# Where a block of normalised activations is written from and how it lies in SBUF, and who adds bias and x to the output, in a ConvNeXt-V2 block on one core

## The chip, the core and the metric

The kernel runs on one core of a Trainium2 chip. A core has five engines with a program each: TensorE (PE in the profile: matrix multiplies; PEld is its weight load), VectorE (DVE), ScalarE (ACT), GpSimd (POOL) and SyncE (SP, which here only issues transfers). They wait for each other through semaphores. Sixteen DMA engines carry transfers between HBM and SBUF, the on-chip memory of 128 partitions. A transfer is issued from the instruction queue of SP, ScalarE or GpSimd, and an instruction that waits holds up everything behind it in its queue. Matrix products land in PSUM, eight banks of 2 KB in each partition.

The metric is the device time of one execution in microseconds (us), the median of several.

## What is computed

One ConvNeXt-V2 block on an image of 512 x 512 pixels with 96 channels, in bfloat16, with 384 hidden channels:

```python
def reference(x, dw, w1, w2, grn_gamma, grn_beta):
    ...
    for i in range(K):
        for j in range(K):
            out = out + xp[:, i:i+H, j:j+W, :] * dw[i, j][None, None, None, :]
    h = _layernorm(out, axis=-1)
    h = jnp.einsum('bhwc,ce->bhwe', h, w1)
    h = _gelu(h)
    gx = jnp.sqrt((h * h).sum(axis=(1, 2), keepdims=True) + 1e-6)
    nx = gx / (gx.mean(axis=-1, keepdims=True) + 1e-6)
    h = grn_gamma * (h * nx) + grn_beta + h
    h = jnp.einsum('bhwe,ec->bhwc', h, w2)
    return x + h
```

The sum of `h * h` runs over the whole image, so nothing of the second product can be finished before every pixel has been through the first one. That cuts the kernel in two phases.

## The kernel before

**Tiles.** The image is cut into 128 blocks of 4 rows (`NBLK`, `GR`). A block is 2048 pixels. `yn` is the convolved and normalised block with rows x 32 channels on the partitions; `ynT` is the same block with channels on the partitions, and it is what the first product reads. The way from the one to the other leads through HBM: `stage_write` writes `yn` to `yn_dram` in four transfers, one for each row of the block, and `stage_read` reads the block back as 96 partitions of 4 KB. There is a ring of six `ynT` tiles; partitions 96 to 127 of them are set to zero once (`setup_ynt`), and so are those rows of the weights `w1p`, so that the product can run over 128 partitions.

**Phase 1** is a loop over slots; in a slot each step is done for another block, by a table (`put`, `get`). A block's way is: load x (`load_x`, four slots ahead), transpose on VectorE (`turn_x`), convolution on TensorE in three bursts (`conv`), evacuation by ScalarE (`evac`, the tile `y_bf`), squares on GpSimd (`stage_sq`), statistics on TensorE, inverse standard deviation for four blocks at a time on GpSimd (`stage_rstd`, `stage_newton`), its way through HBM to all partitions (`stage_rows`, `stage_bcast`), the normalisation on GpSimd (`stage_norm`, one slot later `stage_write`, another slot later `stage_read`), and two slots after that the first product with GELU. In that step `unit(bank, n)` makes n PSUM banks on TensorE and has ScalarE apply GELU from them into the tile `g`; ScalarE does nine such activations and one evacuation in a slot. VectorE then takes the statistics of `g` (BATCH_NORM_STATS2), TensorE the others (`gram_next`). The slots are called steady here when their block for the first product is below `TAIL0` (114).

In phase 1 SP issues all transfers of a slot, in this order: load of x, `stage_read`, `stage_write`, `stage_bcast`, `stage_rows`, and one third of a block of `g` that is kept in HBM (`store_next`). Every instruction on the engines stays in the order of the program (class `InOrder`, line 35, which is why most lines of the profile are L35).

**Phase 2** goes once more over the blocks. For 35 of them `g` is read back from HBM (`gl`, line 290, from GpSimd's queue), for 5 it was held in SBUF, and for 88 it is made again from `ynT` (`recompute`: three matmuls of 512 columns for each quarter of a block, one GELU of 1536 columns); for 85 of these `ynT` is read again from `yn_dram` (line 294, from SP's queue). That read takes 128 rows, the last 32 being the next block's, which meet zero weights. Then, for each block (`stage_mm2`):

- TensorE makes the second product in four parts (`sub`, 0 to 3) of 4 x 96 columns, 12 matmuls each. Two PSUM banks take turns (`out_bank`), so a part needs the bank of the part before the last.
- GpSimd has added x (`xr`, loaded by line 279) and the bias (`B2c`) for the whole block ahead of time (`stage_xb`, line 324, tile `xb`, two blocks ahead; three buffers).
- VectorE adds the PSUM bank and its part of `xb` into `o_sb` (four buffers), and SP stores `o_sb` when the next block is done (`stage_out`, line 352).

`pace` spreads the recomputed quarters evenly between the parts: about two for every three parts.

Of the kernel before, what the change touches and what calls it, by code (L numbers as in the profile page):

```python
# [12 lines left out]
GR = 4  # L13
# [43 lines left out]
def kernel(  # L57
# [52 lines left out]
    def chans(i):  # L110
        return slice(i, 64, 2) if i < 2 else slice(64, 96)
# [10 lines left out]
    def yn_src(q):  # L122
        return yn_dram[q].rearrange("c (r w) -> c r w", r=GR)

    def yn_rows(q):
        return yn_dram[q:q + 2].rearrange("q c (r w) -> (q c) r w", r=GR)[0:128]

# [10 lines left out]
    rowsel = consts.tile([128, GR], bf16, name="rowsel")  # L138
    w1_raw = consts.tile([C, E], bf16, name="w1_raw")
    w1p = consts.tile([128, E], bf16, name="w1p")  # L140
# [43 lines left out]
    with ExitStack() as p1:  # L184
# [68 lines left out]

        cen = consts.tile([C, 128], bf16, name="cen")
        xtpool = pc.enter_context(tc.tile_pool(name="xt", side="right", bufs=1))
# [27 lines left out]
        def load_rest(n, sq, pq):  # L283
            q = ORDER[n]
            v = grp.setdefault(q, {})
            if is_held(q):
                v["g"] = gs[q]
            elif is_whole(q):
                v["g"] = late.gl.tile([128, NQ, NCH, QW], bf16, name="gl")
                pq.dma_start(out=v["g"][:].rearrange("p t j w -> p (t j w)"), in_=g_dram[whole.index(q)])  # L290
            else:
                ynt = yn_ring[SLOTS[nth_made[q] % NYT]]
                if q not in KEPT:
                    sq.dma_start(out=ynt[:], in_=yn_rows(q))
                v["ynt"] = ynt
# [24 lines left out]
        def stage_xb(q, pq, bias):  # L320
            if q is None:
                return
            xb = late.xb.tile([128, PXP, C], f32, name="xb")
            pq.tensor_tensor(out=xb[:], in0=grp[q]["xr"][:],  # L324
                                    in1=bias[:, None, :].to_broadcast([128, PXP, C]), op=ALU.add)
            grp[q]["xb"] = xb

        def stage_mm2(n, q):
# [3 lines left out]
            for sub in range(NSUB):  # L332
                O = out_bank()
                for gl_ in range(GPS):
                    gg = sub * GPS + gl_
                    for j in range(NCH):
                        t, c = gg // GQ, gg % GQ * 128
                        pe.matmul(O[:, gl_, :], lhsT=g[:, t, j, c:c + 128], rhs=W2s[:, j, :],
                                   start=(j == 0), stop=(j == NCH - 1))
                dve.tensor_tensor(out=o_sb[:, sub * GPS:(sub + 1) * GPS, :], in0=O,  # L340
                                   in1=xb[:, sub * GPS:(sub + 1) * GPS, :], op=ALU.add)
                if n == NBLK - 1:
# [44 lines left out]
        pool.memset(cen[:], 1.0)  # L387
        pool.memset(w1p[C:128, :], 0.0)
        dve.memset(SG, 0.0)
# [24 lines left out]
        for i in range(NI):  # L414
            act.dma_start(out=w1_raw[i:C:NI, :], in_=w1[chans(i), :])
        act.dma_start(out=w2_sb[:], in_=w2.rearrange("(j p) c -> p j c", p=128))
# [4 lines left out]
        def setup_ynt():  # L421
            for t in yn_ring:
                pool.memset(t[C:128, :, :].rearrange("p r w -> p (r w)").bitcast(f32), 0.0)

        def setup_mlp():
# [6 lines left out]
            dve.scalar_tensor_tensor(out=w1p[:C, :], in0=w1m[:C], scalar=-1.0 / C, in1=w1_raw[:],  # L432
                                     op0=ALU.mult, op1=ALU.add)
# [207 lines left out]

        def stage_write(b):
            yn = yns.pop(b)
            for r in range(GR):
                sp.dma_start(out=yn_dst(b, r), in_=yn[32 * r:32 * r + 32, :, :])

        def stage_read(b):
            t = yn_ring[b % NYT]
            sp.dma_start(out=t[:C], in_=yn_src(b))
            ynts[b] = t  # L650
# [175 lines left out]
        for s in range(last_slot + 1):  # L826
            get = lambda kind: at.get((s, kind), [])
            if s + 4 < NBLK:
                load_x(s + 4)
            for b in get("read"):  # L830
                stage_read(b)
            for b in get("write"):
                stage_write(b)
            for k in get("bcast"):
                stage_bcast(k)
            for k in get("rows"):
                stage_rows(k)
            store_next()
            for k in get("newton"):
                stage_newton(k, pool)  # L840
# [4 lines left out]
            for k in get("rstd"):  # L845
                stage_rstd(k, pool)
            mlp = get("mlp")

# [36 lines left out]
            else:  # L885
# [4 lines left out]
                conv(0)  # L890
                unit(0, 2)
                unit(2, 1)
                squares(0)
# [4 lines left out]
                unit(3, 1)  # L898
                unit(4, 2)
                squares(1)  # L900
                gram_next(1 if taps else 2)
# [6 lines left out]
                if evac:  # L908
                    evac()
                gram_next(1 if taps else 2)  # L910
                unit(8, 2)
                unit(10, 1)
                for b2 in get("stats"):
# [138 lines left out]
```

## Time and profile before

| what | value |
|---|---|
| three runs | 1480.27, 1486.15, 1486.81 us |
| median of the runs | 1486.15 us |
| span of the profiled execution | 1480.8 us |
| mean granted TensorE clock in it | 0.994 of full speed |
| first matmul of the second product | 974.7 us after the start |
| moved by DMA | 433.08 MB, mean 292 GB/s |
| of it, reads of ynT in phase 2 | 85 of 512 KB |
| writes of yn | 512 of 96 KB |

The profile is that of one execution. Its page gives busy time for each engine and a line for each group of like instructions; the trace behind it has the start and length of every instruction, and from the semaphores it can be told who ended a wait. Busy time is a union: two overlapping instructions of an engine count once, and an engine that is busy all the time isn't always the one that the others wait for. Times within the trace count from its first instruction.

### The profile page before, as it was taken

How to read it: one execution, taken by the hardware profiler on the slowest of the kernel's cores; microseconds unless marked ns; L12 is line 12 of the kernel's file. 1: busy time of each engine (PE TensorE's matmuls, PEld its weight loads, DVE VectorE, ACT ScalarE, POOL GpSimd, SP SyncE). 2: the span in 40 equal slices, each digit the busy share in tenths (PEclk: the TensorE clock that was granted, in tenths of full speed). 3: DMA queues.
4: the chain of work that ended last, by engine and by line, in shares of the span. 5: the costliest groups of instructions: out<-in, count | busy, mean ns of one | idle time of the engine just before them, and what ended most of it. 6: DMA issues, size and time to landing. Idle time of an engine off the chain costs nothing.

```text
span 1480.8 us, 54225 instructions
## 1 busy us (share of the span) xinstructions
PE 1391.3 (94%) x23125; PEld 810.4 (55%) x23125; DVE 1182.0 (80%) x2135; ACT 1414.4 (96%) x1595; POOL 1300.3 (88%) x922
## 2 busy tenths in 40 slices
PE   8888999999999999999999997789999999999998
PEld 3434444444444444444444445467777777776776
DVE  7849989999999999999999987965555555555555
ACT  7888989999999999999999999999999999999997
POOL 3459889998998999998999987569999999999997
PEclk9999999999999999999999999999999999999999
DMA  5568788788888888888888866669999999999997
GB/s 180 179 205 255 241 253 280 228 271 260 260 248 264 258 264 255 276 253 254 263 258 266 263 216 195 195 225 409 366 359 402 417 416 413 419 410 417 411 412 282
DMA packets 167768, 433.08 MB, mean 292 GB/s; under 512 B 31558, under 2 KB 81318, under 8 KB 163046
## 3 DMA queue, kind: packets, MB, share of 16 engines
q1 hardware_dynamic: 151284, 326.04, 66.3%
q0 software_dynamic: 14880, 103.43, 17.6%
q8 instruction: 181, 2.97, 0.8%
q14 instruction: 61, 0.50, 0.1%
q10 hardware_dynamic: 1362, 0.15, 0.1%
HBM read 273.30 MB, written 156.22 MB: 290 GB/s over the span
## 4 chain that ended last, share of the span: by engine, by line
PE 30%; ACT 24%; DMA 19%; POOL 13%; DVE 6%; issue 4%; SPq 4%; POOLq 0%; ACTq 0%; DVEq 0%
PE PS L35 30%; ACT g L35 16%; DMA out_dram<-o_sb 9%; POOL yn L35 6%; ACT y_bf L35 5%; POOL ysq L35 5%; SPq L35 4%; DMA yn_dram<-yn 3%; DVE bst L35 3%; DMA xin<-in_x_dram 2%; DMA rbc<-r_dram 2%; DMA ynT<-yn_dram 1%; DMA g_dram<-g 1%; DVE o_sb L35 1%; ACT xT L35 1%
## 5 line engine op out<-in xcount | busy, mean ns | idle before, releaser
L35 ACT ACTIVATE g<-PS 128x512 bf16<-128x512 f32 (+2 forms) x1062 | 727.7, 864 | 16.5 <-PE PS L35 15.6
L35 DVE BATCH_NORM_STATS2 bst<-g 128x6 f32<-128x512 bf16 x1110 | 671.3, 672 | 35.4 <-ACT g L35 34.5
L35 PE MATMUL PS<-ynT,w1p 128*128 128x512 bf16 x2181 | 609.6, 381 | 23.6 <-ACT g L35 5.4
L35 ACT ACTIVATE gr<-PS 128x1536 bf16<-128x1536 f32 x360 | 498.5, 1459 | 18.8 <-PE PS L35 13.8
L35 POOL TENSOR_TENSOR yn<-y_bf,rbc 128x1536 bf16<-128x1536 bf16 x126 | 391.3, 3108 | 77.3 <-ACT rbc L35 21.9
L35 DVE TENSOR_TENSOR o_sb<-PS,xb 128x384 bf16<-128x384 f32 x512 | 277.3, 556 | 227.0 <-PE PS L35 190.1
L324 POOL TENSOR_TENSOR xb<-xr,B2c 128x1536 f32<-128x1536 bf16 x118 | 368.1, 3133 | 4.3 <-DVE o_sb L35 2.0
L35 PE MATMUL PS<-xT,Wq 64*32 64x511 bf16 (+1 forms) x9198 | 340.5, 389 | 26.2 <-ACT y_bf L35 8.1
L35 POOL TENSOR_TENSOR ysq<-y_bf 128x1536 bf16<-128x1536 bf16 x114 | 313.6, 2752 | 12.8 <-ACT y_bf L35 12.8
L35 PEld LDWEIGHTS <-w1p 128*128 128x128 bf16 x2181 | 171.6, 98 | 222.0 <-issue 133.4
L35 PEld LDWEIGHTS <-gr 128*128 128x128 bf16 x4296 | 212.1, 98 | 68.9 <-issue 12.0
L35 PE MATMUL PS<-W2s,gr 128*128 128x96 bf16 x4224 | 223.5, 206 | 8.2 <-DVE o_sb L35 8.0
L35 PEld LDWEIGHTS <-Wq 64*32 64x32 bf16 x9216 | 111.9, 90 | 193.3 <-issue 145.9
L35 ACT ACTIVATE y_bf<-PS 128x1536 bf16<-128x1536 f32 (+2 forms) x135 | 199.4, 1482 | 17.4 <-PE PS L35 13.3
L35 DVE STREAM_TRANSPOSE xT<-xin 128x576 f32<-128x576 f32 (+1 forms) x256 | 181.4, 748 | 8.1 <-DMA xin<-in_x_dram 8.1
L35 PEld LDWEIGHTS <-g 128*128 128x128 bf16 x1704 | 104.9, 98 | 86.3 <-issue 54.3
L35 PE MATMUL PS<-w1p,ynT 128*128 128x256 bf16 (+2 forms) x822 | 125.8, 273 | 8.0 <-ACT xT L35 3.2
L35 PE MATMUL PS<-g 128*128 128x128 bf16 x1464 | 122.6, 220 | 2.9 <-DVE PS L35 2.6
L35 PEld LDWEIGHTS <-gl 128*128 128x128 bf16 x1680 | 82.8, 98 | 26.8 <-issue 5.0
L35 PE MATMUL PS<-W2s,gl 128*128 128x96 bf16 x1680 | 89.5, 206 | 3.4 <-DVE o_sb L35 3.2
L35 PEld LDWEIGHTS <-ynT 128*128 128x128 bf16 x822 | 64.1, 97 | 31.5 <-issue 13.7
L279 POOL DMA_DIRECT2D xr<-in_x_dram x115 | 63.7, 555 | 14.2 <-POOL xb L324 14.2
(105 smaller groups left out, 576.5 us busy)
## 6 DMA issues: line engine op xcount, KB each, us to landing
xin<-in_x_dram SPq DMA_DIRECT2D x126, 432.0 KB
g_dram<-g SPq DMA_DIRECT2D x105, 512.0 KB
gl<-g_dram POOLq DMA_DIRECT2D x35, 1536.0 KB, 11.3
yn_dram<-yn SPq DMA_DIRECT2D x512, 96.0 KB
ynT<-yn_dram SPq DMA_DIRECT2D x128, 384.0 KB
out_dram<-o_sb SPq DMA_DIRECT2D x127, 384.0 KB
xr<-in_x_dram POOLq DMA_DIRECT2D x123, 384.0 KB, 6.9
ynT<-yn_dram SPq DMA_DIRECT2D x85, 512.0 KB
```

Of the source, the lines that this page charges most:

```text
L35: r = f(*a, **k)
L279: pq.dma_start(out=xr[:], in_=x[0, r0:r0 + GR].rearrange("r w c -> (r w) c").rearrange("(p g) c -> p g c", g=PXP))
L324: pq.tensor_tensor(out=xb[:], in0=grp[q]["xr"][:], in1=bias[:, None, :].to_broadcast([128, PXP, C]), op=ALU.add)
```

## The change

It has three parts.

1. **Layout of ynT.** Channel 3c+i goes to partition 4c+i instead of 3c+i. So three of every four partitions hold a channel and each fourth holds zero. A read is three transfers of 32 partitions (i = 0, 1, 2), in both phases; in phase 2 the next block's rows are no longer read. The weights `w1_raw` are laid out alike, and the ring's tiles are set to zero in all partitions.
2. **Queue of the writes.** In steady slots the four writes of `yn` are issued from ScalarE's queue, one each after the activations of unit(0, 2), unit(4, 2), the evacuation and unit(8, 2). SP's order in these slots becomes: load of x, broadcasts, rows, store, reads. In the other slots all stays on SP, reads first.
3. **The adds of phase 2.** GpSimd makes `xb` for the first three parts only. For the fourth VectorE first adds the bias to the PSUM bank in place, then adds x out of the bank into `o_sb`. `xr` is thus in use until VectorE's last add and has six buffers instead of five.

```diff
-    def yn_src(q):
-        return yn_dram[q].rearrange("c (r w) -> c r w", r=GR)
-
-    def yn_rows(q):
-        return yn_dram[q:q + 2].rearrange("q c (r w) -> (q c) r w", r=GR)[0:128]
+    def yn_src(q):
+        return yn_dram[q].rearrange("(c i) (r w) -> i c r w", i=NI, r=GR)
+
+    def read_yn(eng, t, q):
+        for i in range(NI):
+            eng.dma_start(out=t[i:128:4], in_=yn_src(q)[i])
...
                 if q not in KEPT:
-                    sq.dma_start(out=ynt[:], in_=yn_rows(q))
+                    read_yn(sq, ynt, q)
...
         def stage_xb(q, pq, bias):
-            xb = late.xb.tile([128, PXP, C], f32, name="xb")
-            pq.tensor_tensor(out=xb[:], in0=grp[q]["xr"][:],
-                                    in1=bias[:, None, :].to_broadcast([128, PXP, C]), op=ALU.add)
+            n = PXP - GPS
+            xb = late.xb.tile([128, n, C], f32, name="xb")
+            pq.tensor_tensor(out=xb[:], in0=grp[q]["xr"][:, :n, :],
+                                    in1=bias[:, None, :].to_broadcast([128, n, C]), op=ALU.add)
...
+                add = xb
+                if sub == NSUB - 1:
+                    dve.tensor_tensor(out=O, in0=O, in1=B2c[:, None, :].to_broadcast([128, GPS, C]), op=ALU.add)
+                    add = grp[q]["xr"]
                 dve.tensor_tensor(out=o_sb[:, sub * GPS:(sub + 1) * GPS, :], in0=O,
-                                   in1=xb[:, sub * GPS:(sub + 1) * GPS, :], op=ALU.add)
+                                   in1=add[:, sub * GPS:(sub + 1) * GPS, :], op=ALU.add)
...
-            act.dma_start(out=w1_raw[i:C:NI, :], in_=w1[chans(i), :])
+            act.dma_start(out=w1_raw[i:128:4, :], in_=w1[chans(i), :])
...
-                pool.memset(t[C:128, :, :].rearrange("p r w -> p (r w)").bitcast(f32), 0.0)
+                pool.memset(t[:].rearrange("p r w -> p (r w)").bitcast(f32), 0.0)
...
-        def stage_write(b):
+        def write_parts(b, eng):
             yn = yns.pop(b)
-            for r in range(GR):
-                sp.dma_start(out=yn_dst(b, r), in_=yn[32 * r:32 * r + 32, :, :])
+            return [lambda r=r: eng.dma_start(out=yn_dst(b, r), in_=yn[32 * r:32 * r + 32, :, :]) for r in range(GR)]
 
         def stage_read(b):
             t = yn_ring[b % NYT]
-            sp.dma_start(out=t[:C], in_=yn_src(b))
+            read_yn(sp, t, b)
...
-            for b in get("read"):
-                stage_read(b)
-            for b in get("write"):
-                stage_write(b)
+            mlp = get("mlp")
+            steady = bool(mlp) and mlp[0] < TAIL0
+            wparts = [f for b in get("write") for f in write_parts(b, act if steady else sp)]
+            if not steady:
+                for b in get("read"):
+                    stage_read(b)
+                while wparts:
+                    wparts.pop(0)()
...
             store_next()
+            if steady:
+                for b in get("read"):
+                    stage_read(b)
...
                 unit(0, 2)
+                write_next()
...
                 unit(4, 2)
+                write_next()
...
                 if evac:
                     evac()
+                write_next()
                 gram_next(1 if taps else 2)
                 unit(8, 2)
+                write_next(len(wparts))
...
-                late.xr = p2.enter_context(tc.tile_pool(name="xr", side="right", bufs=5))
+                late.xr = p2.enter_context(tc.tile_pool(name="xr", side="right", bufs=6))
```

More of the change, by code (lines that the diff above doesn't have):

```diff
@@ L138 @@
     rowsel = consts.tile([128, GR], bf16, name="rowsel")
-    w1_raw = consts.tile([C, E], bf16, name="w1_raw")
+    w1_raw = consts.tile([128, E], bf16, name="w1_raw")
     w1p = consts.tile([128, E], bf16, name="w1p")
@@ L252 @@
             dve.tensor_copy(out=eye32[32 * q:32 * q + 32, :], in_=ident_f[32 * q:32 * q + 32, 32 * q:32 * q + 32])
-        cen = consts.tile([C, 128], bf16, name="cen")
+        cen = consts.tile([128, 128], bf16, name="cen")
         xtpool = pc.enter_context(tc.tile_pool(name="xt", side="right", bufs=1))
@@ L387 @@
         pool.memset(cen[:], 1.0)
-        pool.memset(w1p[C:128, :], 0.0)
+        pool.memset(w1_raw[:], 0.0)
         dve.memset(SG, 0.0)
@@ L431, in setup_mlp @@
                           start=(j == 0), stop=(j == NCH - 1))
-            dve.scalar_tensor_tensor(out=w1p[:C, :], in0=w1m[:C], scalar=-1.0 / C, in1=w1_raw[:],
+            dve.scalar_tensor_tensor(out=w1p[:], in0=w1m, scalar=-1.0 / C, in1=w1_raw[:],
                                      op0=ALU.mult, op1=ALU.add)
@@ L838, with write_next @@
             store_next()
+            if steady:
+                for b in get("read"):
+                    stage_read(b)
+            def write_next(n=1):
+                for f in wparts[:n]:
+                    f()
+                del wparts[:n]
             for k in get("newton"):
@@ L846 @@
                 stage_rstd(k, pool)
-            mlp = get("mlp")
             def spread_out():
```

## The prediction, made before the changed kernel was run

> **What bounds the kernel now.** First the page's summary, then busy time in windows (start:end, then for each engine busy us and instruction count, TensorE clock, DMA share, GB/s): one from the steady part of phase 1, one from phase 2.
>
> ```profile
> PE 1391.3 (94%) x23125; PEld 810.4 (55%) x23125; DVE 1182.0 (80%) x2135; ACT 1414.4 (96%) x1595; POOL 1300.3 (88%) x922
> ...
> 300.00:360.00 60.00, 58.02 (x1058) 29.23 (x1056) 59.80 (x103) 60.00 (x86) 56.43 (x42) 1.00 0.82 256
> ...
> 1200.00:1260.00 60.00, 58.19 (x852) 42.96 (x850) 32.60 (x61) 57.29 (x42) 58.04 (x37) 1.00 1.02 414
> ```
>
> In phase 1 ScalarE has no idle time at all and VectorE 0.2 of 60 us: a slot (one block) lasts 7.03 us and ScalarE sets it. In phase 2 ScalarE, GpSimd, the DMA engines and TensorE all stand near full, VectorE at 54%. A busy share doesn't tell which one sets the end there, so I read the timeline (start, length, engine, operation):
>
> ```profile
> 1200.12 1.18 PE L35 MATMUL PS<-W2s,gl 128*128 128x96 bf16 x24
> ...
> 1200.84 1.07 DVE L35 TENSOR_TENSOR o_sb<-PS,xb 128x384 bf16<-128x384 f32 x2 [0.60 <-PE PS L35]
> ...
> 1201.14 0.81 PE L35 MATMUL PS<-ynT,w1p 128*128 128x512 bf16 x3
> ...
> 1201.79 0.67 PE L35 MATMUL PS<-W2s,gr 128*128 128x96 bf16 x12
> ...
> 1202.30 0.81 PE L35 MATMUL PS<-ynT,w1p 128*128 128x512 bf16 x3
> 1202.56 0.56 DVE L35 TENSOR_TENSOR o_sb<-PS,xb 128x384 bf16<-128x384 f32 x1 [0.66 <-PE PS L35]
> ...
> 1202.95 1.18 PE L35 MATMUL PS<-W2s,gr 128*128 128x96 bf16 x24
> ```
>
> From start to start TensorE takes 42.5 ns for a 96-wide matmul (1200.12 to 1201.14, 24 of them) and 216 ns for a 512-wide one (1201.14 to 1201.79, three), with nothing between. Phase 2 holds 6144 of the one and, after its first, 1038 of the other: 261 + 225 = 486 us. By the trace its matmuls run from 974.7 to 1477.1, 502.4 us. So **TensorE sets phase 2**, and some 16 us of it are waits. Which ones (waiter, what ended the wait, total us, times, longest):
>
> ```profile
> DVE o_sb L35 <- DMA out_dram<-o_sb: 35.4, 24, 2.7
> ...
> PE PS L35 <- DVE o_sb L35: 11.3, 15, 1.6
> ```
>
> VectorE waits for an output buffer whose store hasn't landed; the sum's PSUM bank stays full and TensorE stands still, 11.3 us in all. The DMA engines are full (1.02).
>
> **The change, part by part.**
>
> *Second add in phase 2.* In one part of four VectorE now adds the bias into the PSUM bank, then x out of it. The single add takes 0.556 us (group mean). No row has VectorE both reading and writing a 384-wide PSUM tile, so I take the same 0.556, and 0.034 us from the dependent chain of small VectorE operations at 969 to 971 us, where each starts that long after the end of the one it needs. The bank is held 0.59 us longer. VectorE has the time (128 x 0.556 = 71 us of some 230 idle), but there are two banks: the group after next needs this one. In the timeline above the pair at 1200.84 frees its first bank at 1201.40, and the group that needs it starts at 1201.79: slack 0.39. The add ending at 1203.12 frees a bank needed at 1203.46 (second half of the x24): 0.34. The second of the pair ends at 1201.91 for a group at 1202.95: 1.04. Taking from the trace all 127 last adds of a block against the group after next, 96 have 0.40 us or less and 31 have 1.05. Where TensorE does wait, it starts 0.053 us after the add's end (the smallest slack). So a wait of 0.59 + 0.053 - 0.398 = 0.245 us, 96 times: **+23.5 us**, on the engine that sets the end. Ends: 0.50 us (two adds at the pitch of an independent pair) gives +15; 0.75 (PSUM output a third dearer) gives +39. The last block's extra add lengthens the tail by **+0.6**.
>
> *Less for GpSimd.* Its add shrinks from 1536 to 1152 columns.
>
> ```profile
> L324 POOL TENSOR_TENSOR xb<-xr,B2c 128x1536 f32<-128x1536 bf16 x118 | 368.1, 3133 | 4.3 <-DVE o_sb L35 2.0
> ```
>
> With 0.30 us for 64 columns (var) as the other point, 1152 cost 2.39 us: 0.74 us less, 125 times. VectorE waits 0.9 us in all for xb, so this pays **0** by itself. Its worth is in what comes next: GpSimd's period is 3.95 us a block against TensorE's bare 486/128 = 3.80, so it would have capped any recovery. x is now held until VectorE's last add; a sixth buffer covers this, and GpSimd's load of x five blocks on waits for an event 1 us from the one its own add awaits now. **0**, ends 0 and +5.
>
> *Smaller reads in phase 2.* 85 reads go from 512 to 384 KB: 10.9 MB, 26 us at 416 GB/s, but only the 11.3 us of waits can be paid back. Per block the traffic becomes 189 MB/128 = 1.48 MB, in 4.0 us 370 GB/s against 416 at saturation, so I take the waits as gone: **-11.3**. Other end 0: each read becomes three issues on SP, and hardware DMAs take turns on eight semaphores (the trace shows the turn), so an issue waits for the landing of the eighth before it, now under three blocks back instead of five.
>
> *yn writes on ScalarE's queue.* 110 steady slots, 4 issues each. SP's row, and two from ScalarE's start-up:
>
> ```profile
> 312.05 2.49 SPq L35 DMA_DIRECT2D yn_dram<-yn  x4
> ...
> 5.59 0.59 ACTq L35 DMA_DIRECT2D w_raw<-in_w_dram  x1
> 5.77 0.88 ACT L35 ACTIVATE Wq<-g 32x288 bf16<-32x288 bf16 x2
> ...
> 11.63 0.38 ACTq L35 DMA_DIRECT2D bet_bf<-in_grn_beta_dram  x1
> 12.06 1.45 ACT L35 ACTIVATE y_bf<-PS 128x1536 bf16<-128x1536 f32 x1 [4.16 <-DMA gam_bf<-in_grn_gamma_dram]
> ```
>
> An issue takes 0.6 us of the queue. At 5.59 activations that stand ahead of it in the program run beside it: the queue goes on while the engine works. In the slot the four issues stand behind activations of 1024 or 1536 columns (0.9 and 1.33 us from start to start), so I cost them at **0**; the cover is 0.3 us each, and without it 440 x 0.6 = 264 us would fall on ScalarE. What isn't covered is a wait, as at 11.63: that issue waited for the semaphore last used by SP's load at 7.89, and ScalarE stood 4.16 us. Behind a waiting write stand all later activations, behind them TensorE's PSUM banks. (a) The first write needs yn. Setting the end of each yn against the start of the slot that will write it, yn is late in 30 of 108 slots: 5.9 us at worst near 115 us, later up to 3.9 and mostly under 1. Summed, 33 us beyond the cover; but a ScalarE that waits lets GpSimd (56 of 60 busy) catch up for good, so it is paid about once, and near 120 us the trace already has 4.9 us of ScalarE idle for the same lateness. **+1**, ends 0 and +33. (b) The shared semaphores: in slots with broadcasts the first write follows that slot's broadcast. **+2**, ends 0 and +25. The Trainium skill (DMA: Bandwidth & Descriptors, Anatomy of one DMA) states that a DMA's semaphore wait happens on the issuing sequencer before dispatch, so it speaks against a queue that sets the slot; if every late yn were paid, that rule would make (a) 33 instead of 1.
>
> *SP in phase 1* loses 2.5 us of issues a slot and gains two reads (0.7), and its broadcasts no longer stand behind writes that wait.
>
> ```profile
> SPq L35 <- DMA yn_dram<-yn: 133.5, 149, 3.8
> ...
> SPq L35 <- POOL yn L35: 64.3, 39, 4.2
> ```
>
> ScalarE's idle time from 240 to 900 us, beyond two gaps of its own, is 7 us (at 694 to 699 and 887 to 897, behind GpSimd). I take **-2**: ends -7 and 0.
>
> *Layout.* Three reads of 32 partitions for one of 96; the memset and the w1 setup keep their columns: **0**, since a read has two slots of lead. The skill (SBUF — State Buffer, Summary: rules for kernel authors) asks for 128 partitions and one DMA, not several; its fixed 2 us a DMA would make three reads in a row about 7 us by estimate, and that stays inside two slots, so the sum is the same by both.
>
> **Sum.** 23.5 + 0.6 - 11.3 + 1 + 2 - 2 = +13.8 on the profiled 1480.8: 1494.6. Three runs have 1480.27, 1486.15 and 1486.81, so the profiled execution is 5.3 below the median; the forecast is 1494.6 + 5.3 = **1500**.
>
> **Rivals.** *Faster:* the two adds end within 0.345 us of today's one (the slack less 0.053), so the banks don't bind, and both DMA waits and the 7 us in phase 1 go: 1486 - 11.3 - 7 = 1468. For it: full DMA engines, SP's long waits. Against: a second add of 0.556 us on a slack of 0.40. *No change:* the bank costs 15 and the waits go, with -2 to -7 in phase 1: 1486 + 15 - 11 - 4 + 1 = 1487. *ScalarE blocked:* writes wait once per four slots for yn or a broadcast, about 1 us in 27 groups, on top of the forecast: 1500 + 27 = 1527. For it: the 4.16 us at 12.06, and that late yn comes in every fourth slot. Against: paid-once lateness.
>
> **How the numbers follow.** About 0.5% (7 us) is what this kernel's runs can tell from no change. Forecast 0.47, ScalarE blocked 0.15, no change 0.19, faster 0.19. Slower 0.62, same 0.19, faster 0.19. Range 1470 to 1522: the low end near the faster rival, the high end the bank at +39 with the DMA waits gone, most of the blocked case's lower part in it; the forecast's own range is 1490 to 1512.
>
> **What would show it.** Right: in phase 2 two adds per last part, the second 0.03 us behind the first; TensorE's wait for VectorE up from 11 to over 20 us, in some 100 pieces of 0.25; waits for output stores nearly gone; DMA share under 0.95; GpSimd no longer full. In phase 1 slots of 7.03 us still, ScalarE's queue issuing beside its activations. Wrong: no small TensorE waits (the bank isn't the bound), output waits as before (semaphores), or slots longer than 7.1 us (ScalarE blocked).

## The result and the profile after

| | before | after |
|---|---|---|
| median of six runs each | 1483.32 us | 1600.92 us |
| lowest to highest | 1480.26 to 1486.81 | 1588.79 to 1603.57 |
| span of the profiled execution | 1480.8 us | 1598.2 us |
| first matmul of the second product | 974.7 us | 1076.1 us |
| last matmul of the second product | 1477.1 us | 1594.0 us |
| mean slot in the middle of phase 1 | 7.10 us | 7.96 us |

The ratio is 1.0768 with a 95% interval of 1.0737 to 1.0800: the change makes the kernel 7.7% slower. The forecast was 1500 us with a range up to 1522, so the sign was right and the size was not. Of the 117.4 us between the two spans, phase 2 holds 15.5 (517.9 in place of 502.4 from its first matmul of the second product to its last), the tail 0.5, and **phase 1 holds 101.4**, where the forecast had put +1.

The view of windows that the prediction used, of the changed kernel: the same window in phase 1, and one in its later phase 2 (columns as there: start:end, length, busy us and count of PE, PEld, DVE, ACT, POOL, then clock, DMA share, GB/s):

```profile
300.00:360.00 60.00, 53.61 (x952) 26.06 (x950) 55.15 (x95) 54.34 (x76) 50.99 (x40) 0.97 0.80 245
1300.00:1360.00 60.00, 59.00 (x846) 42.84 (x845) 40.45 (x75) 57.59 (x42) 44.72 (x35) 1.00 1.00 382
```

In phase 1 every engine has become idler: ScalarE, which had no idle time, now has 5.7 us of 60, and even the DMA engines carry less. No engine took over as the bound, so a wait did. In phase 2 VectorE has more to do and GpSimd less (58 to 45 of 60), as the change intends. The DMA engines stay full there (1.00), where the prediction named a share under 0.95 as a sign of being right.

The waits of the changed kernel (waiter, what ended the wait, total us, times, longest):

```profile
PE PS L35 <- ACT g L35: 82.6, 108, 3.5
...
ACT g L35 <- PE PS L35: 35.1, 51, 1.6
ACT g L35 <- DMA ynT<-yn_dram: 31.6, 24, 3.4
ACT g L35 <- DMA g_dram<-g: 8.3, 7, 1.6
...
ACT g L35 <- DMA xin<-in_x_dram: 6.6, 3, 3.5
...
PE PS L35 <- DVE o_sb L35: 5.7, 9, 1.1
...
DVE o_sb L35 <- DMA out_dram<-o_sb: 2.4, 3, 1.2
```

The last two lines answer to the two waits shown before: VectorE's wait for output stores is gone (35.4 to 2.4 us). Of the others the first two have grown (from 10.8 and 15.6 us) and the three waits for DMAs are new. These three look odd: an activation that fills `g` reads PSUM and needs no read of `ynT`, no store of `g` and no load of x. It doesn't wait for them itself. The timeline shows who does (start, length; ACTq and SPq are the two issuing queues):

```profile
612.67 1.21 ACTq L35 DMA_DIRECT2D yn_dram<-yn  x2
613.40 0.77 SPq L35 DMA_DIRECT2D xin<-in_x_dram  x1
613.47 3.04 ACT L35 ACTIVATE g<-PS 128x1024 bf16<-128x1024 f32 x4
614.26 0.39 SPq L35 DMA_DIRECT2D g_dram<-g  x1
615.57 0.56 ACTq L35 DMA_DIRECT2D yn_dram<-yn  x1
616.41 2.00 ACT L35 ACTIVATE g<-PS 128x512 bf16<-128x512 f32 x3
618.69 1.78 SPq L35 DMA_DIRECT2D ynT<-yn_dram  x2
618.96 0.57 ACTq L35 DMA_DIRECT2D yn_dram<-yn  x1
619.59 0.60 ACT L35 ACTIVATE g<-PS 128x512 bf16<-128x512 f32 x1 [1.18 <-DMA xin<-in_x_dram]
```

The second write of a block starts at 618.96 (the two at 612.67 are the third and fourth of the block before it, the one at 615.57 is this block's first). The trace's semaphore updates have the load of x that SP issued at 613.40 landing at 618.942, and both use the same one of the eight semaphores that the hardware DMAs, those of SP and ScalarE, take in turn. So the write, whose data had long been there, waited for a load that has nothing to do with it, and the activation behind it stood 1.18 us. From 240 to 900 us ScalarE is idle for 66.7 us, against 7.9 before; 55.8 us of it, in 57 pieces, stand directly behind a write that its semaphore had just let go.

SP is held the other way round, by its data: between 614.26 and 618.69 it issues nothing, because the next read of `ynT` needs the four writes of its block in HBM, and the last of them, issued by ScalarE at 613.30, landed at 618.538. From 240 to 900 us 72 of 83 blocks' reads wait so, and SP stands 236.7 us for writes of `yn` (88.1 before). Over the whole run SP's row, shown for the kernel before with 133.5 us, is:

```profile
SPq L35 <- DMA yn_dram<-yn: 345.0, 141, 8.1
```

So each queue waits for the other: a late write holds SP's reads and the loads behind them, and a late load holds the next write through the turn. From 240 to 900 us, 145 of the 331 writes on ScalarE's queue start within 0.2 us of the landing of the DMA that last used their semaphore, 60 of these behind one of the reads of `ynT`. In the kernel before, with one queue, the DMA that last used a semaphore is always the eighth before (771 of 771 issues); with two queues that drift against each other it lies 3 to 14 issues back. It isn't late `yn`: in this trace `yn` is ready 4 to 11 us before its first write is issued.

The timeline of phase 2, at the last part of one block:

```profile
1301.17 1.18 PE L35 MATMUL PS<-W2s,gr 128*128 128x96 bf16 x24
1301.88 0.57 DVE L35 TENSOR_TENSOR PS<-PS,B2c 128x384 f32<-128x384 f32 x1 [0.60 <-PE PS L35]
1302.19 0.81 PE L35 MATMUL PS<-ynT,w1p 128*128 128x512 bf16 x3
1302.48 0.56 DVE L35 TENSOR_TENSOR o_sb<-PS,xr 128x384 bf16<-128x384 f32 x1
1302.95 0.55 DVE L35 TENSOR_TENSOR o_sb<-PS,xb 128x384 bf16<-128x384 f32 x1
1303.09 0.67 PE L35 MATMUL PS<-W2s,gr 128*128 128x96 bf16 x12
```

The bias add takes 0.57 us, the add of x starts 0.03 us behind it and ends at 1303.04, and the matmuls that need this bank start 0.05 us later. Three matmuls of 512 columns from 1302.19 would have been through at 1302.84; TensorE stands 0.25 us. Phase 2 has 99 such pieces of 0.2 to 0.3 us, 25.3 us in all, against 3 before. The view of waits doesn't put them down to VectorE (5.7 us above), since by the rows it is the weight load that stands still there; in phase 2 its line grows from 17.8 us in 28 pieces to this:

```profile
PEld L35 <- issue: 39.3, 110, 1.4
```

### The profile page after: what moved, and what is told of

It is laid out like the page before. It is cut to its first block, busy times and chain, and to the rows that moved or that the text cites. A ratio compares the mean times of both kernels' runs of the same rounds, so it can differ in the third digit from the quotient of the medians.

```text
span 1598.2 us, 55080 instructions
## 1 busy us (share of the span) xinstructions
PE 1425.6 (89%) x23125; PEld 818.6 (51%) x23125; DVE 1268.8 (79%) x2263; ACT 1435.5 (90%) x1595; POOL 1203.1 (75%) x922
## 5 line engine op out<-in xcount | busy, mean ns | idle before, releaser
L35 DVE BATCH_NORM_STATS2 bst<-g 128x6 f32<-128x512 bf16 x1110 | 680.0, 673 | 121.7 <-ACT g L35 120.6
L35 PE MATMUL PS<-ynT,w1p 128*128 128x512 bf16 x2181 | 623.9, 386 | 100.6 <-ACT g L35 70.0
L35 ACT ACTIVATE gr<-PS 128x1536 bf16<-128x1536 f32 x360 | 504.2, 1450 | 33.3 <-PE PS L35 25.4
L35 PE MATMUL PS<-xT,Wq 64*32 64x511 bf16 (+1 forms) x9198 | 347.4, 396 | 29.4 <-ACT y_bf L35 14.9
L326 POOL TENSOR_TENSOR xb<-xr,B2c 128x1152 f32<-128x1152 bf16 x118 | 280.5, 2391 | 102.0 <-DMA xr<-in_x_dram 74.5
L35 DVE TENSOR_TENSOR o_sb<-PS,xb 128x384 bf16<-128x384 f32 x384 | 210.9, 556 | 110.1 <-PE PS L35 89.6
L35 ACT ACTIVATE y_bf<-PS 128x1536 bf16<-128x1536 f32 (+2 forms) x135 | 191.4, 1423 | 15.1 <-PE PS L35 11.0
L35 PE MATMUL PS<-w1p,ynT 128*128 128x256 bf16 (+2 forms) x822 | 127.5, 274 | 15.7 <-ACT g L35 9.6
L35 DVE TENSOR_TENSOR PS<-PS,B2c 128x384 f32<-128x384 f32 x128 | 72.5, 567 | 57.0 <-PE PS L35 57.0
```

The costliest lines, as they stand in the source:

```text
L35: r = f(*a, **k)
L326: pq.tensor_tensor(out=xb[:], in0=grp[q]["xr"][:, :n, :], in1=bias[:, None, :].to_broadcast([128, n, C]), op=ALU.add)
```

## The experiments

The expectations name theories by letters. **S**: a write on ScalarE's queue waits until the hardware DMA that last had its semaphore, the eighth before it in the turn and often one of SP's, has landed, and ScalarE's activations wait behind it. **Y**: writes wait for late `yn`. **I**: ScalarE pays for issuing itself. **R**, later sharpened to **Q** and **N**: the three reads cost, because SP's queue fills and the statistics' broadcast behind them comes late (N: by the number of issues, not the layout). **B**: the second add holds the PSUM bank. **G**: GpSimd caps what phase 2 can give back. Three rounds each unless told otherwise; ratios are against runs of the kernel before on the same chip, with 95% intervals. Lengths of phases come from one profiled execution each. In seven of these kernels phase 2 is as before, and it takes 501.5 to 507.5 us; in six phase 1 is, and it takes 973.5 to 982.8. Smaller differences than these say nothing.

### The parts of the change alone

**ScalarE's queue alone** (the kernel before with the steady writes of `yn` on ScalarE's queue, at the changed kernel's places, and with its order on SP, the read last):

```diff
-                sp.dma_start(out=yn_dst(b, r), in_=yn[32 * r:32 * r + 32, :, :])
+            return [lambda r=r: eng.dma_start(out=yn_dst(b, r), in_=yn[32 * r:32 * r + 32, :, :]) for r in range(GR)]
...
+            wparts = [f for b in get("write") for f in write_parts(b, act if steady else sp)]
```

> The kernel before with one part of the change: the steady writes of yn on ScalarE's queue, in the new order on SP. Layout, single reads of 96 rows and phase 2 are the old ones. Theory S (hardware transfers take turns on eight semaphores, so a write in ScalarE's queue waits for the landing of a transfer that SP issued, and ScalarE stands): the slot has 9 transfers here against 11 with the three reads, so the waits are there but fewer; slots between 7.03 and 7.99 us, the run 20 to 80 us slower than before (1500 to 1565). Theory Y (writes wait in ScalarE's queue for GpSimd's yn): layout plays no part, slots as in the changed kernel, near 7.99 us, the run 90 to 100 us slower. Theory R (three reads and their later issue load SP, and the blocks come late; the queue of the writes costs nothing): slots 7.0 to 7.1 us, the run within 8 us of before.

Measured: 1549.42 us, ratio 1.0418 (1.0384 to 1.0452); phase 1 is 57.5 us longer (second product from 1032.2), the mean slot 7.64 us. 108 of 344 writes start within 0.2 us of the landing that frees their semaphore, and of ScalarE's 49.6 us of idle time from 240 to 900 us 44.4 stand directly behind such a write. Time and slot lie in the ranges of S alone. The move of the queue costs more than four times what the forecast summed for the whole change. The new order on SP has no run of its own; below, reads put last make a kernel faster, not slower.

**All but ScalarE's queue** (the changed kernel with the writes on SP):

```diff
-            steady = bool(mlp) and mlp[0] < TAIL0
+            steady = False
```

> The changed kernel with the steady writes of yn back on SP, reads first, as before; three reads per block, the new layout and phase 2 stay changed. Theory S: no write stands in ScalarE's queue, phase 1 falls back to slots of 7.0 to 7.3 us (SP still has two more issues a slot, and shorter turns), the run 15 to 40 us slower than before, of which phase 2 is 15. Theory Y: the same as S. Theory R: SP now has the three reads and the writes, so slots are at least as long as in the changed kernel, 8 us or more, and the run is 110 us or more slower.

Measured: 1568.19 us, ratio 1.0541 (1.0505 to 1.0576); phase 1 longer by 63.9 us, phase 2 by 15.5. Neither theory had this. The layout with three reads, which the forecast cost at 0, costs as much in phase 1 as the queue does, by another way: most slots last 7.08 us, nearly as before, and about one in six lasts 8 to 12.5. Three waits of this kernel:

```profile
POOL yn L35 <- DMA rbc<-r_dram: 83.3, 19, 12.3
ACT g L35 <- PE PS L35: 53.3, 52, 2.5
...
PE PS L35 <- POOL ysq L35: 41.7, 24, 3.2
```

GpSimd waits for the broadcast of the statistics (before: 21.8 us in 9 waits), its squares come late, TensorE waits for these and ScalarE for TensorE.

**The second add alone** (the kernel before with the adds of phase 2 split as in the change, and six buffers of x):

```diff
+                if sub == NSUB - 1:
+                    dve.tensor_tensor(out=O, in0=O, in1=B2c[:, None, :].to_broadcast([128, GPS, C]), op=ALU.add)
+                    add = grp[q]["xr"]
```

> The kernel before with phase 2's adds alone: GpSimd makes xb for three parts, VectorE adds bias and x itself in the fourth, six buffers of x; the reads stay at 512 KB. Theory B (the second add holds a PSUM bank 0.25 us too long in about 96 blocks, and TensorE sets phase 2): phase 2 grows by 24 us less what falls together with waits for output stores; the run 12 to 26 us slower than before. Rival (VectorE has the time, so the add is free and only GpSimd is relieved): within 5 us of before.

Measured: 1508.91 us, ratio 1.0142 (1.0112 to 1.0172); phase 2 525.2 in place of 502.4, so **+22.8** against a forecast of +23.5, with 98 pieces of 0.2 to 0.3 us. Theory B stands. Below it lies a wait that the forecast had priced at 0: GpSimd now waits for x, whose buffers VectorE holds longer.

```profile
POOL xb L325 <- DMA xr<-in_x_dram: 94.3, 28, 5.4
DVE o_sb L35 <- POOL xb L325: 16.0, 15, 2.3
```

**The smaller read in phase 2 alone** (96 rows of 4 KB in one DMA in place of 128):

```diff
-                    sq.dma_start(out=ynt[:], in_=yn_rows(q))
+                    sq.dma_start(out=ynt[:C], in_=yn_src(q))
```

> The kernel before with phase 2 reading 96 rows in one transfer (384 KB for 512 KB), nothing else. If the waits for output stores in phase 2 come from full DMA engines: they nearly vanish, 8 to 13 us faster than before. If they come from something else (GpSimd's pace, order on SP's queue): within 3 us of before.

Measured: 1508.52 us, ratio 1.0132 (1.0096 to 1.0167), a miss: less is read and phase 2 takes 524.6 us, 22 more. First the waits of this kernel, then one window of 60 us in phase 2 (columns as above):

```profile
DVE o_sb L35 <- DMA out_dram<-o_sb: 65.4, 37, 3.8
PE PS L35 <- DVE o_sb L35: 28.1, 26, 2.7
```

```profile
1200.00:1260.00 60.00, 56.38 (x823) 41.67 (x820) 31.42 (x59) 55.43 (x41) 55.31 (x36) 1.00 1.02 372
```

The DMA engines are as full as before (1.02) and move 372 GB/s in place of 414: the packets of 4 KB take 195 ns on the mean in place of 165, those of the loads of x 279 in place of 244. Bytes were the wrong measure of what a read takes from the DMA engines. Why a read of 96 partitions makes packets longer, these runs don't tell.

### What couples the two queues

**Two more turns beside ScalarE's writes** (ScalarE's queue alone, and two DMAs of 4 bytes on SP in each steady slot; they write to a tile that nobody reads):

```diff
+                for k in range(2):
+                    sp.dma_start(out=turn_dram[2 * s + k], in_=zrow[0:1, 0:2])
```

> The kernel before with the four yn writes a block on ScalarE's queue, and on SP two more DMAs of 4 bytes in each steady slot, behind the read. They move nothing that counts; they take two turns of the eight semaphores and about 0.6 us each of SP's queue, which has idle time. Theory S: the eighth before a write now lies nearer, more writes wait: slots from 7.64 towards the 7.96 us of the changed kernel, 1570 to 1605 us. Theory I: ScalarE issues as much as without them, 1545 to 1555 us.

Measured: 1586.00 us, ratio 1.0695 (1.0658 to 1.0733), 37 us more than without the two, and phase 1 ends at 1079.2, as in the changed kernel (1076.1). 159 of 326 writes now start as their semaphore comes free. ScalarE's idle time behind a freed write goes from 44.4 to 66.2 us (240 to 900). Two DMAs that carry nothing cost as much as the two reads a slot that the change adds. Theory S forecast 1570 to 1605, theory I 1545 to 1555.

**The control: the same two turns with all writes on SP.**

> The kernel before, all writes on SP, with two more DMAs of 4 bytes on SP in each steady slot (the control to the two added beside writes on ScalarE's queue, which cost 37 us there). Theory S: in one queue a turn that is waited for holds only SP, which has time: 1483 to 1497 us. If two more DMAs a slot cost by themselves: 1515 us or more.

Measured: 1491.63 us, ratio 1.0033 (1.0006 to 1.0061): 5 us by the interval's middle, 12 of phase 1 in the profiled execution. The same DMAs cost some seven times less where the turn is waited for in one queue that has time. Together the two runs show that what costs is not the two DMAs by themselves but that ScalarE stands in the turn.

**Four writes as one DMA on ScalarE's queue**:

```diff
-            return [lambda r=r: eng.dma_start(out=yn_dst(b, r), in_=yn[32 * r:32 * r + 32, :, :]) for r in range(GR)]
+            return [lambda: eng.dma_start(out=yn_all(b), in_=yn[:])]
```

> The kernel before with the steady yn writes on ScalarE's queue, but the four writes of a block as one DMA of 384 KB, at the place of the first. Theory S (the writes wait for the eighth hardware DMA before them, which is often one of SP's that has not landed): with about 4.7 hardware DMAs a slot in place of 7.7 the eighth before lies more than a slot back and has landed; slots back to 7.05 to 7.15 us, 1485 to 1497 us. Theory I (ScalarE pays for each issue, about 0.14 us of the 62 us for each of 440): a quarter of the 62 us, 1503 us.

Measured: 1706.41 us, ratio 1.1510 (1.1465 to 1.1555). Both theories missed, and one reason is that the DMA became another one: its slowest dimension is the 4 rows, it raises its semaphore by five updates in place of sixteen, and it lands after 11.5 us (median) in place of 4.0. The Trainium skill (DMA: Bandwidth & Descriptors, Why a DMA increments its semaphore by 16 and not by 1) says that a DMA is split over the largest number of engines up to 16 that divides the slowest dimension of both its sides; with 4 there the trace agrees. What it shows for S is the other direction: with DMAs that take three times as long to land, ScalarE stands behind the turn for up to 6 us. How much of the loss that is, this run doesn't tell: TensorE was also at half clock for 170.7 of the 900 us from 100 to 1000.

```profile
503.60 0.53 ACTq L35 DMA_DIRECT2D yn_dram<-yn  x1
504.18 2.98 ACT L35 ACTIVATE g<-PS 128x512 bf16<-128x512 f32 x5 [6.12 <-DMA ynT<-yn_dram]
```

**All four writes late in the slot** (ScalarE's queue alone, without the first three places):

```diff
-                write_next()
...
                 unit(8, 2)
                 write_next(len(wparts))
```

> The kernel before with the steady yn writes on ScalarE's queue, all four at the last of the four places, behind eleven twelfths of the slot's units (at 1549 us they stood at four places from the first units on). Theory S (a write waits for SP's DMAs of the same slot to land): these have had 5 us and more to land, so few writes wait: slots from 7.64 to 7.1 to 7.35 us, 1490 to 1520 us. Theory I (the price is that of issuing on ScalarE's queue): 1545 to 1555 us, or more, since four issues in a row have less cover.

Measured: 1664.14 us, ratio 1.1199 (1.1153 to 1.1245), a miss. The turn did what S said: only 34 of 304 writes start as their semaphore comes free. But two other prices came up. The timeline of this kernel:

```profile
512.88 0.56 ACTq L35 DMA_DIRECT2D yn_dram<-yn  x1
513.36 1.02 ACT L35 ACTIVATE g<-PS 128x1024 bf16<-128x1024 f32 x1
513.48 2.06 ACTq L35 DMA_DIRECT2D yn_dram<-yn  x3
515.58 4.88 ACT L35 ACTIVATE g<-PS 128x512 bf16<-128x512 f32 x8 [1.21 <-PE PS L35]
```

Three issues in a row, 2.06 us, stand behind one activation of 1.02, and the engine is idle for 1.21 (the view names TensorE, but the activation starts 0.04 us after the third issue ends); even the quickest slots (the twentieth part) take 7.74 us, where with spread writes they take 6.95. And a late write holds its `yn` buffer: from 240 to 900 us GpSimd waits 94.6 us for the three of them. How the loss splits between the two wasn't measured. As far as the quickest slots show, theory I holds for issues in a row, and the cover of which the forecast spoke holds for issues that are spread.

### What the three reads cost where SP writes

**Three reads of neighbouring rows** (the kernel before, its read of 96 partitions cut in three, no other layout):

```diff
-            sp.dma_start(out=t[:C], in_=yn_src(b))
+            for i in range(NI):
+                sp.dma_start(out=t[32 * i:32 * i + 32], in_=yn_src(b)[32 * i:32 * i + 32])
```

> The kernel before with its read of 96 partitions in phase 1 as three reads of 32 neighbouring partitions (the changed kernel reads every fourth partition), all on SP. Theory N (three issues take SP 1.8 us a slot in place of 0.44, which fills its queue and makes the statistics' broadcast late): phase 1 longer by 40 to 65 us, 1525 to 1552 us. If it is the layout of the changed kernel that costs: 1483 to 1500 us.

Measured: 1539.41 us, ratio 1.0357 (1.0323 to 1.0390), phase 1 longer by 53.2 us. Theory N stands: most of it is the number of reads. The rest up to 63.9 us, 10.7, is little more than the spread; if it is the layout's, SP's row says how: an issue takes 0.325 us for 96 rows, 0.419 for 32 neighbouring ones and 0.587 for every fourth of 128 (medians).

**The three reads behind the broadcasts** (all but ScalarE's queue, and in SP's order writes, broadcasts, rows, then reads):

```diff
-                for b in get("read"):
-                    stage_read(b)
...
             for k in get("rows"):
                 stage_rows(k)
+            if not steady:
+                for b in get("read"):
+                    stage_read(b)
```

> The changed kernel with the yn writes back on SP (1568 us), and there the three reads put behind the broadcasts and rows of the slot in place of ahead of them. Theory Q (three reads cost SP 1.8 us a slot instead of 0.4 and hold the rows and the broadcast of the statistics behind them, so that GpSimd's yn comes late, once in four slots): phase 1 recovers most of its 55 us, 1515 to 1540 us. If the reads cost through the DMA engines or the semaphores instead: 1560 to 1575 us.

Measured: 1550.18 us, ratio 1.0451 (1.0393 to 1.0510): 18 us better, not the 28 to 53 of theory Q, and outside both ranges. Order is part of it. The rest is, as far as its queue shows, that SP is full: its issues take 571 of the 660 us from 240 to 900, against 453 before. How late the statistics come can be read from the trace, from the end of VectorE's transpose (`rt`) to the landing of the last of the four broadcasts (medians of 21 to 23), beside the mean slot:

| kernel | statistics' way | mean slot |
|---|---|---|
| before | 15.7 us | 7.10 us |
| two more turns, writes on SP | 17.1 | 7.24 |
| three reads behind the broadcasts | 18.5 | 7.43 |
| three reads of neighbouring rows | 18.7 | 7.50 |
| all but ScalarE's queue | 19.2 | 7.56 |
| ScalarE's queue alone | 11.7 | 7.64 |
| changed kernel | 13.8 | 7.96 |

Where SP writes, the slot follows this way. Where ScalarE writes, the way is shorter than before and the slot longest: the changed kernel's loss is not late statistics.

### What phase 2 could give back

**The changed kernel without its second add**:

```diff
-            n = PXP - GPS
-            xb = late.xb.tile([128, n, C], f32, name="xb")
+            xb = late.xb.tile([128, PXP, C], f32, name="xb")
...
-                if sub == NSUB - 1:
-                    dve.tensor_tensor(out=O, in0=O, in1=B2c[:, None, :].to_broadcast([128, GPS, C]), op=ALU.add)
-                    add = grp[q]["xr"]
```

> The changed kernel with phase 2's adds as before (GpSimd adds the bias to all four parts), its three reads of 32 partitions kept. Theory B (the second add held the PSUM bank, 15 to 23 us): phase 2 from 517.9 to 495 to 503 us, 1578 to 1586 us in all. If the three reads cost as the one read of 96 partitions did (21 us): phase 2 at 515 to 525 us, 1598 to 1608 us.

Measured: 1582.21 us, ratio 1.0670 (1.0621 to 1.0719), phase 2 501.0: theory B again, 16.9 us. What matters more is that phase 2 is no shorter than before the change, within the spread (1.4 us), although the store waits are gone:

```profile
DVE o_sb L35 <- POOL xb L325: 52.8, 60, 3.2
...
DVE o_sb L35 <- DMA out_dram<-o_sb: 1.6, 2, 0.9
```

VectorE waits for GpSimd's add instead.

**Five output buffers** (the kernel before):

```diff
-                late.o = p2.enter_context(tc.tile_pool(name="o", side="right", bufs=4))
+                late.o = p2.enter_context(tc.tile_pool(name="o", side="right", bufs=5))
```

> The kernel before with five output buffers in phase 2 in place of four. The prediction took the waits for output stores (35 us of VectorE, 11.3 us of TensorE) as waits that more transfer rate would end. If they are jitter that a buffer covers: 8 to 13 us faster, 1472 to 1479 us, and this beats both kernels. If the DMA engines' rate sets them, the next wait takes their place: 1482 to 1490 us.

Measured: 1478.82 us, ratio 0.9963 (0.9941 to 0.9984), phase 2 496.9. **This one beats both kernels**, the one before by 0.4%. The time lies at the end of the range for jitter, the gain of 5.8 us is about half of the 8 to 13 that it was to bring. Its waits show the same exchange:

```profile
DVE o_sb L35 <- POOL xb L324: 44.6, 55, 1.5
PE PS L35 <- DVE o_sb L35: 5.5, 18, 0.3
DVE o_sb L35 <- DMA out_dram<-o_sb: 1.0, 2, 0.5
```

**Bias of the fourth part added by VectorE in SBUF** (five output buffers, six of x; five rounds):

```diff
+                if sub == 0:
+                    xv = late.xv.tile([128, GPS, C], f32, name="xv")
+                    dve.tensor_tensor(out=xv[:], in0=grp[q]["xr"][:, PXP - GPS:, :],
+                                      in1=B2c[:, None, :].to_broadcast([128, GPS, C]), op=ALU.add)
```

> The kernel before with five output buffers and six of x in phase 2, GpSimd adding bias and x of three parts in four as in the changed kernel, and VectorE adding those of the fourth part in SBUF, behind its first sum of the block, so that no PSUM bank is held longer. Theory G (with the store waits gone GpSimd's add of 1536 columns is what VectorE waits for, 45 to 53 us, and it capped what phase 2 could give back): phase 2 from 496.9 (five output buffers alone) to 487 to 493 us, those waits under 10 us, 1469 to 1476 us in all, faster than both kernels. If GpSimd is not the cap: 1477 to 1481 us as with five output buffers alone.

Measured: 1494.89 us, ratio 1.0071 (1.0050 to 1.0093), phase 2 513.6: a miss. The groups of this kernel (busy us, mean ns of one, idle before):

```profile
L35 DVE TENSOR_TENSOR xv<-xr,B2c 128x384 f32<-128x384 bf16 x128 | 173.5, 1355 | 0.0
L35 DVE TENSOR_TENSOR o_sb<-PS,xv 128x384 bf16<-128x384 f32 x128 | 71.4, 558 | 42.8 <-PE PS L35 42.7
```

An add of 384 columns with both inputs in SBUF takes 1355 ns, with one in PSUM 558. GpSimd no longer holds VectorE up, but this add does.

**x loaded from SP's queue in phase 2** (five output buffers, GpSimd's add whole; five rounds):

```diff
-                load_xr(n + PRE, pq)
+                load_xr(n + PRE, sq)
```

> The kernel before with five output buffers in phase 2 and the loads of x there issued on SP in place of GpSimd, whose add keeps all four parts. GpSimd's period per block is then its add of 3.13 us without the 0.55 us of the issue; nothing is added on VectorE or in PSUM. Theory G (GpSimd caps phase 2 once the store waits are gone): VectorE's waits for xb from 44.6 to under 10 us, phase 2 from 496.9 to 487 to 492 us, 1468 to 1475 us. If the DMA engines' rate is the cap: store or load waits come back in their place, phase 2 at 495 to 500 us, 1476 to 1483 us.

Measured: 1482.01 us, ratio 0.9975 (0.9950 to 1.0000), phase 2 497.9.

```profile
POOL xb L324 <- DMA xr<-in_x_dram: 28.7, 13, 3.8
DVE o_sb L35 <- DMA out_dram<-o_sb: 26.6, 21, 2.6
...
DVE o_sb L35 <- POOL xb L324: 0.7, 1, 0.7
```

GpSimd is relieved (0.7 us of waits) and nothing is gained, since the waits for transfers come back: of the two ranges it is that of the DMA engines' rate. The reading that fits both runs is that GpSimd and the DMA engines both stand near 497 us, and taking away one shows the other.

## Why the prediction was wrong, and where it was right

**The step that failed** is the term "(b) The shared semaphores", priced at +2 with ends 0 and +25, and beside it the layout at 0, "since a read has two slots of lead". Phase 1 measured +57.5 us for the queue alone and +101.4 with the three reads. The prediction had seen the mechanism at 11.63 us, where an issue waited for the semaphore of a load that SP had issued, and ScalarE stood 4.16 us. It then looked only at one place where a write might follow a fresh DMA, the slots with broadcasts. But the turn goes round in any slot: some 8.3 hardware DMAs a slot before, and 10.4 with two more reads, pass through eight semaphores, and these DMAs take 3 to 5 us to land (medians by kind in the changed kernel). So what a write waits for was issued about a slot ago or less. And it closes a loop that no term had: SP's reads wait for the block's writes, which stand behind activations in ScalarE's queue, and what SP issues late lands late for the next writes. The rule that the prediction set against the change, the Trainium skill's (DMA: Bandwidth & Descriptors, Anatomy of one DMA) that the wait is on the issuing sequencer, agrees with the 1.18 us at 619.59; it had been applied to the wait for `yn`, not to that for the turn.

**Layout at 0** failed by what it counted. A read's lead covers its landing; it doesn't cover three places in SP's order and in the turn. "Two reads (0.7)" of SP's time measured three issues of 0.587 us for one of 0.325, about 1.4 us a slot. With writes on SP this fills the queue and delays the statistics (+53.2 us by number, +63.9 with layout); with writes on ScalarE it takes two turns, which alone cost the 37 us of the empty DMAs.

**Late `yn`** (a): the small price was right, and partly by luck. `yn` is early, since a slower slot gives GpSimd time, as the prediction argued; but what slowed the slot was the turn, not the late `yn`.

**SP's relief, -2**: the statistics' way did shorten (15.7 to 11.7 us with ScalarE's queue alone), but it wasn't what held the slot any more.

**The issue at 0**: holds for spread issues (quickest slots of 6.95 us), fails for issues in a row.

**The second add, +23.5**: right in mechanism and in size: +22.8 alone, within a spread of some us; in the changed kernel the 99 small pieces make 25.3 us.

**Store waits, -11.3**: they went (35.4 to 2.4 us), as forecast, but not for that price. TensorE's other stalls in phase 2 fell from 14.5 to 7.3 us, so 7 came back beside the second add; with the second add undone the whole phase gained nothing beyond the spread. The reason given, fewer bytes, is not shown: with the read of 96 rows fewer bytes went with longer waits (65.4 us), and what ended them in the changed kernel stays open. "GpSimd's period ... would have capped any recovery" was said of the kernel without the change's relief, and the trace without the second add shows it. Its 3.95 us a block is the mean spacing of GpSimd's adds, waits included; the work itself is 3.13 us for the add, 0.55 for the issue of x and 0.55 for that of `g` in 35 of 128 blocks, some 3.83 us.

**GpSimd's add of 1152 columns, 2.39 us**: right (2.39 us in the trace).

**x held longer, 0**: GpSimd waited 74.5 us for x in the changed kernel; VectorE waited 8.8 us for GpSimd, so little of it reached TensorE.

**The rivals.** "ScalarE blocked" named the right place and direction. Its price came from one wait in four slots, 27 us; in the changed kernel nearly every second write waits (145 of 331).

## What to carry to other kernels

Before a transfer moves to the queue of an engine that sets the pace, write down what each of its issues can wait for, the turn of shared semaphores included: count the DMAs that pass between a transfer and the one whose semaphore it takes, and compare their time to land with the time between the two. Write down, too, what on the old queue waits for the moved transfer. Splitting one transfer into three is paid in issue time and turns, which bytes and leads don't show. And where two limits lie close together, as GpSimd and the DMA engines here, the waits of one hide the other, so that a wait's total is no estimate of what its removal gives.

## What the runs showed of the hardware

**Idle time and the clock.** From 100 to 1000 us the records have TensorE at half clock for 4 stretches, 13.7 us in all, before, and for 14, 58.0 us, after. Beside such a stretch 24 matmuls of the convolution take 1.48 us in place of 0.88:

```profile
551.12 0.88 PE L35 MATMUL PS<-xT,Wq 64*32 64x512 bf16 x24
...
556.98 0.59 PE L35 MATMUL PS<-ynT,w1p 128*128 128x512 bf16 x2 [2.05 <-ACT g L35]
559.17 0.59 PE L35 MATMUL PS<-ynT,w1p 128*128 128x512 bf16 x1 [1.60 <-ACT g L35]
559.68 1.48 PE L35 MATMUL PS<-xT,Wq 64*32 64x512 bf16 x24
```

The stretch runs from 557.79 to 564.62: it begins after one wait for ScalarE, of 2.05 us, and within the next, of 1.60. All 14 stretches after begin behind 3.4 us in which TensorE was idle for 1.4 to 2.8 us. With three reads of neighbouring rows the 9 slots from 240 to 900 us that touch half clock last 10.65 us on the mean, the others 7.20. How much of these slots is the clock and how much the wait ahead of it wasn't taken apart, so the 101 us may hold a share of it. By estimate that share is at most 22 us, half of the 44 us of half clock that came with the change; with ScalarE's queue alone, 20.5 us of half clock in place of 13.7, it is at most 3.4 of the 57.5.

**VectorE beside GpSimd.** The add of 384 columns in SBUF takes 548 to 550 ns in the four cases where no add of GpSimd runs in that time, and 949 to 3558 ns wherever one overlaps for half of it or more. The Trainium skill (SBUF — State Buffer, SBUF: two separate sides) says that the two share a pair of ports which one holds for a whole instruction, also where VectorE has two inputs in SBUF; these runs agree. With an input in PSUM the add stays at 0.54 to 0.57 us in every kernel.

**Issue time** of a DMA on SP depends on its shape, 0.28 us for 4 bytes, 0.325 for 96 rows of 4 KB, 0.587 for 32 rows that lie four partitions apart.
